# Weight preparation, value loads and planned order of a fused top-k attention and FFN kernel

## The chip, the cores and the metric

The kernel runs on one core of a Trainium2 chip. The core has TensorE (PE; its weight loads are PEld in the profile), VectorE (DVE), ScalarE (ACT), GpSimd (POOL) and SyncE (SP), which here issues all DMA. The metric is the device time of one execution in microseconds, as the median of several runs.

## What is computed

Attention that keeps the 32 largest scores of each row, for 4 batches of 8 heads, 576 positions and 64 columns a head, and then two FFNs over the 2304 tokens.

```python
scores = scale * np.matmul(q, k.transpose(0, 1, 3, 2))
kth = np.partition(scores, -top_k, axis=-1)[..., -top_k:-top_k + 1]
scores = np.where(scores >= kth, scores, -1000000000.0)
attn = np.exp(scores - np.max(scores, axis=-1, keepdims=True))
attn = attn / (np.sum(attn, axis=-1, keepdims=True) + 1e-09)
x = np.matmul(attn, v)
h = x @ w_in;  x = np.maximum(0.01 * h, h) @ w_out
h = x @ w_in2
g = np.where(h >= 1, h, np.where(h <= -1, 0.0, (h + 1) ** 2 / 4.0))
return g @ w_out2
```

The inner width of an FFN is 2048, the outer 512. The result is float32.

## The kernel before

**Units.** Each batch's head has 512 queries in two halves of 256 (`a` = 0, 1) and 64 that are left over. A unit ("m") is one head and one half: scores on PE (L688), copied to SBUF by ACT (tile `s`), the top-k on DVE with four MAX8 (L736) and three MATCH_REPLACE8 (L740) for each of two tiles of 128 queries, the exponential on ACT (`e`, L755 and L756), the division by the sum on POOL (L763), the transposes on PE (L775, copied by ACT to `ptr`), and the product with the values on PE (L859, `pv`). Batch 0 runs all heads of the first half before those of the second, and so loads its values twice. In batches 1 to 3 both halves of a head follow each other. Scores of left-over queries are computed early (`scores_kept`, L712) and come back from DRAM in "r" units. For batches 2 and 3 the transposed left-over rows wait in `rk` and `re` and join the product of the second half (`own` in `pv`).

**Numbers.** PE multiplies a short float type (float32r), so an operand is cut into a high part (ACT casts) and a low one (POOL subtracts): `split`, whose instructions carry L491 and L507. Heads of batches 0 and 1 (`lean_of`) keep their values in float32: `v_whole` loads 128 columns that hold one head's 64 columns twice, and the unit copies out the half that it needs.

**Weights.** The weights arrive as 64-bit floats, 32 blocks of 128 x 512 for each of the two FFNs (layers `L` 0 and 1). `prep_w` makes float32 of each: ACT scales the upper word into `va` (L577), with the exponent placed so that a shift by 3 puts it where it belongs; ACT writes 16 further bits of the mantissa into `bits` (L579); POOL writes the sign, as 0 times the value in bfloat16, into the upper half of `bits` (L584); DVE shifts `va` and joins both (L590). Then the block is cut in two (`px`) and written to DRAM (`scr`). `va` lies in a PSUM bank for the first 16 blocks of layer 0 and in `wa` after that. `bits` is a tile `wb`, of which there are two; it is free again when POOL's subtraction has read it.

**FFN.** `Rows` multiplies rows of batches 0 to 2 (L1032 to L1034 and L1104 to L1106); its activations go through `gt`, of which there are three. `Wide` takes the 768 rows of batch 3 and of the left-over queries at the end, with seven products in place of eight; its first weights come from sums (DVE, L1297) and lie in `ts`, whose first two places are `tsn` and the other three the buffers of `gt`. `late_split` (L1354) writes into the places of `x`.

**Order.** Every operation is recorded with an engine, a duration and the tiles it uses; `Plan.run` then puts them in order before anything is issued. `forward` simulates the engines with given priorities; `backward` gives new priorities from the time that each operation has to the end. Eight passes are made and the shortest kept. Its durations are constants such as `t_a`, `t_v` and 700 for the joining instruction (L592).

## Time and profile before

| | us |
|---|---|
| median of 3 runs | 1146.84 (1146.72 to 1147.48) |
| the profiled execution | 1147.63 |
| its span, first to last instruction | 1145.8 |
| PE busy | 1098.5 (96%) |
| DVE busy | 929.6 (81%) |
| ACT busy | 895.6 (78%) |
| POOL busy | 831.8 (73%) |
| bytes moved by DMA | 251.11 MB, 219 GB/s on average |

Busy time is the union of the instructions that the profiler saw on an engine. Matmuls overlap each other, so the time from the start of one to the start of the next says what one costs, not its duration. Waits are put down to what ended last. Shares over the whole span average over stages with different limits: attention with the first rows of the FFN up to about 860 us, the wide FFN after that.

### The profile page before, as it was taken

How to read it: one execution, taken by the hardware profiler on the slowest of the kernel's cores; microseconds unless marked ns; L12 is line 12 of the kernel's file. 1: busy time of each engine (PE TensorE's matmuls, PEld its weight loads, DVE VectorE, ACT ScalarE, POOL GpSimd, SP SyncE). 2: the span in 40 equal slices, each digit the busy share in tenths (PEclk: the TensorE clock that was granted, in tenths of full speed). 3: DMA queues.
4: the chain of work that ended last, by engine and by line, in shares of the span. 5: the costliest groups of instructions: out<-in, count | busy, mean ns of one | idle time of the engine just before them, and what ended most of it. 6: DMA issues, size and time to landing. Idle time of an engine off the chain costs nothing.

```text
span 1145.8 us, 18836 instructions
## 1 busy us (share of the span) xinstructions
PE 1098.5 (96%) x5992; PEld 959.5 (84%) x5992; DVE 929.6 (81%) x1826; ACT 895.6 (78%) x2029; POOL 831.8 (73%) x952
## 2 busy tenths in 40 slices
PE   6777997999999999999999999999999999999998
PEld 3556896999888788888888888888888999999987
DVE  7999999999999999999999999999947442047510
ACT  6889999999999898989897899999864543346541
POOL 3445587987799878978777777978779884659721
PEclk9899998999999999999999999999999999999999
DMA  9879897789576647564555464544447654755555
GB/s 330 294 268 334 269 392 265 270 307 378 187 269 229 242 164 221 181 216 161 192 177 202 150 204 147 165 146 135 140 149 263 196 201 167 249 211 182 168 169 179
DMA packets 81778, 251.11 MB, mean 219 GB/s; under 512 B 9104, under 2 KB 21520, under 8 KB 77584
## 3 DMA queue, kind: packets, MB, share of 16 engines
q1 hardware_dynamic: 81680, 249.93, 63.5%
q8 instruction: 47, 0.77, 0.3%
q14 instruction: 51, 0.42, 0.1%
HBM read 206.90 MB, written 42.99 MB: 218 GB/s over the span
## 4 chain that ended last, share of the span: by engine, by line
PE 69%; DVE 14%; ACT 9%; POOL 3%; issue 3%; DMA 1%; SPq 0%; POOLq 0%; ACTq 0%; DVEq 0%
PE bank L1034 14%; PE bank L1032 14%; PE bank L1033 14%; DVE m L736 7%; DVE wk L740 5%; PE bank L859 5%; PE bank L775 4%; PE bank L688 4%; PE bank L1104 3%; PE bank L1105 3%; PE bank L1106 3%; PE bank L1381 2%; PE bank L1382 2%; DVE wb L590 2%; PE bank L1380 2%
## 5 line engine op out<-in xcount | busy, mean ns | idle before, releaser
L736 DVE MAX8 m<-wk 128x8 f32<-128x576 f32 x432 | 308.8, 747 | 0.3
L740 DVE MATCH_REPLACE8 wk<-m,wk 128x576 f32<-128x576 f32 x288 | 212.2, 743 | 0.0
L1032 PE MATMUL bank<-x,ring 128*128 128x512 f32 (+2 forms) x376 | 143.1, 381 | 0.0
L507 POOL TENSOR_TENSOR gt<-gr,gt 128x512 fp32r<-128x512 f32 x96 | 126.9, 1322 | 21.6 <-ACT gt L491 12.3
L1034 PE MATMUL bank<-x,ring 128*128 128x512 f32 (+2 forms) x376 | 137.8, 366 | 0.0
L1033 PE MATMUL bank<-x,ring 128*128 128x512 f32 (+2 forms) x376 | 137.7, 366 | 0.0
L507 POOL TENSOR_TENSOR pt<-ptr,pt 64x128 fp32r<-64x128 f32 (+1 forms) x128 | 111.8, 878 | 26.5 <-ACT pt L491 21.7
L763 POOL TENSOR_SCALAR e<-e,rc 128x576 f32<-128x576 f32 x144 | 109.5, 771 | 17.5 <-DVE rc L761 15.5
L491 ACT COPY s<-bank 128x288 f32<-128x288 f32 x256 | 96.8, 402 | 23.4 <-PE bank L688 21.8
L756 ACT ACTIVATE e<-e,nb 128x576 f32<-128x576 f32 x144 | 111.6, 779 | 2.8 <-POOL nb L749 2.7
L775 PE MATMUL bank<-idt,e 128*128 128x128 f32 (+2 forms) x680 | 104.5, 278 | 9.6 <-POOL e L763 7.2
L736 DVE MAX8 m<-s 128x8 f32<-128x576 f32 x144 | 103.4, 745 | 8.6 <-ACT s L491 8.6
L493 ACT ACTIVATE e<-s,nb 128x576 f32<-128x576 f32 x144 | 108.0, 779 | 1.5
L775 PEld LDWEIGHTS bank<-idt,e 128*128 128x128 f32 (+2 forms) x680 | 82.4, 140 | 28.9 <-POOL e L763 11.7
L740 DVE MATCH_REPLACE8 wk<-m,s 128x576 f32<-128x576 f32 x144 | 106.1, 742 | 0.0
L491 ACT COPY ptr<-bank 128x512 f32<-128x512 f32 (+3 forms) x208 | 97.4, 495 | 11.1 <-PE bank L775 10.3
L688 PE MATMUL bank<-kk,qh 128*128 128x288 f32 x384 | 83.5, 311 | 8.3 <-ACT ptr L491 5.9
L507 POOL TENSOR_TENSOR px<-wb,px 128x512 fp32r<-128x512 f32 x58 | 76.6, 1328 | 17.0 <-ACT px L491 16.8
L859 PE MATMUL bank<-ptr,vl 116*128 116x256 f32 (+1 forms) x320 | 81.6, 395 | 4.6 <-ACT ptr L491 4.4
L688 PEld LDWEIGHTS bank<-kk,qh 128*128 128x128 f32 x384 | 66.1, 191 | 21.0 <-ACT ptr L491 6.9
L1034 PEld LDWEIGHTS bank<-x,ring 128*128 128x128 f32 x376 | 70.7, 188 | 10.8
L1032 PEld LDWEIGHTS bank<-x,ring 128*128 128x128 f32 x376 | 70.8, 188 | 7.3 <-ACT gr L493 0.2
(173 smaller groups left out, 3280.6 us busy)
## 6 DMA issues: line engine op xcount, KB each, us to landing
ring<-scr SPq DMA_DIRECT2D x244, 512.0 KB, 3.7
scr<-px SPq DMA_DIRECT2D x58, 512.0 KB, 4.5
wraw<-in_moe_w_in_dram SPq DMA_DIRECT2D x16, 1024.0 KB, 7.1
wraw<-in_moe_w_out_dram SPq DMA_DIRECT2D x16, 1024.0 KB, 7.1
vl<-in_vd_dram SPq DMA_DIRECT2D x24, 320.0 KB, 5.3
kraw<-in_km_dram SPq DMA_DIRECT2D x24, 288.0 KB, 5.0
qraw<-in_qm_dram SPq DMA_DIRECT2D x24, 256.0 KB, 4.3
kraw<-in_km_dram SPq DMA_DIRECT2D x16, 320.0 KB, 4.4
```

What stands on the lines that cost most here:

```text
L491: nc.scalar.copy(out=out_(), in_=in_())
L507: lambda: nc.gpsimd.tensor_tensor(out=out_(), in0=in0(), in1=in1(), op=ALU.subtract),
L688: nc.tensor.matmul(ps()[:, 0:HALF], lhsT=qh()[:, at] if plain else qh()[:, part, at], rhs=kk()[:, c0 + c * HALF:c0 + (c + 1) * HALF], star ...
L736: vec(lambda i=i, c=c, src=src: nc.vector.max(out=m()[:, i, c], in_=src()), 664, [(m, (i, r))], [src], pr)
L740: vec(lambda i=i, c=c, src=src, w=ws[i]: nc.vector.match_replace(out=w(), in_to_replace=m()[:, i, c], in_values=src(), imm_value=NEG), 720 ...
L756: P.op("A", 763, lambda i=i, at=at: nc.scalar.activation(out=at(), in_=at(), func=ACTF.Exp, bias=nb()[:, i, 2:3], accum_out=sums()[:, i:i ...
L763: P.op("P", T_NORM, lambda i=i: nc.gpsimd.tensor_scalar(out=e2()[:, i * S:(i + 1) * S], in0=e2()[:, i * S:(i + 1) * S], scalar1=rc()[:, i: ...
L775: nc.tensor.transpose(ps()[0:n, i * 128:(i + 1) * 128], refs[0][0]()[:, c:c + n], idt())
L859: nc.tensor.matmul(out_ps()[:, at], lhsT=vt()[0:lean_rows[j] if lean else KB, j, :], rhs=src(), start=k == 0 and z == 0, stop=k == len(ste ...
L1032: nc.tensor.matmul(ps, lhsT=wh, rhs=xh, start=first, stop=False, skip_group_check=True)
L1033: nc.tensor.matmul(ps, lhsT=wh, rhs=xl, start=False, stop=False, skip_group_check=True)
L1034: nc.tensor.matmul(ps, lhsT=wl, rhs=xh, start=False, stop=last, skip_group_check=True)
```

## The change

- `prep_w`: ACT's scaling becomes a Prelu whose slope for negative values is 2^32, which leaves a bit in the exponent that the shift by 3 moves into the sign's place. POOL's sign instruction goes, for both layers. The low bits go into one of two fixed tiles (`lows`), in turn, whose other halves are zeroed once at the start. The joined block goes to `wa` (three buffers instead of two, and `va` itself outside PSUM); `wb` is no longer a ring of buffers.
- `v_whole` loads the values of heads 2c and 2c+1 side by side, for the even head, and the odd head uses the same tile. `vl` has three buffers instead of four.
- `pv` with `own`: ACT copies the 64 columns of the left-over rows into the tile of the last keys, and one matmul of 320 columns takes the place of one of 64 and one of 256.
- The planner: two gates (`done`) tell it that `ts` in the buffers of `gt`, and `late_split` in those of `x`, come after their last earlier use. `run` makes 21 forward passes, with factors on the durations of ACT, DVE and POOL in `backward` that differ from pass to pass (`CHAIN`). `forward` and `backward` are written anew in part (what waits for a buffer is set aside until one is freed), with the same rules.

```diff
-BUFS = dict(x=2, xraw=2, kk=4, vl=4, vv=4, kraw=3, px=8, vraw=2, qraw=3, qh=2, s=6, wk=3, e=2, m8=3, nb=3, sums=2, rc=2,
-            pt=3, ptr=3, xb=2, rk=4, re=2, t=3, gr=2, gt=3, wraw=2, wa=2, wb=2)
+BUFS = dict(x=2, xraw=2, kk=4, vl=3, vv=4, kraw=3, px=8, vraw=2, qraw=3, qh=2, s=6, wk=3, e=2, m8=3, nb=3, sums=2, rc=2,
+            pt=3, ptr=3, xb=2, rk=4, re=2, t=3, gr=2, gt=3, wraw=2, wa=3)
...
-EARLY = ("wraw", "wa", "wb", "px")
+EARLY = ("wraw", "wa", "px")
...
-T_SIGN = 795
-SIGNP = (0, 1)
...
+    def done(self, tag):
+
+        uses = {i for i, o in enumerate(self.ops) for r in o[6] if r.tag == tag}
+        self.ops.append(("X", 0, lambda: None, 0.0, uses, [], []))
+        return len(self.ops) - 1
...
     def run(self):
+        self.links()
         prio = [o[3] for o in self.ops]
-        refs = {ref for o in self.ops for ref in o[6] if ref.tag in self.bufs}
-        self.span = None
-        for _ in range(PASSES):
-            for ref in refs:
-                ref.slot = None
+        best = None
+        for z in range(len(CHAIN) + 1):
             span, order = self.forward(prio)
-            if self.span is None or span < self.span:
-                self.span, self.order = span, order
-                slots = [(ref, ref.slot) for ref in refs]
-            began = {i: t for t, i in order}
-            prio = self.backward(began)
+            if best is None or span < best[0]:
+                best = span, order, [(ref, ref.slot) for ref in self.holder]
+            if z < len(CHAIN):
+                prio = self.backward({i: t for t, i in order}, dict(zip("AVP", CHAIN[z])))
+        self.span, self.order, slots = best
...
+CHAIN = (
+    (1.0, 1.0, 1.0), (1.011, 1.025, 0.896), (1.081, 0.936, 1.0), (1.081, 1.033, 1.032), (1.0, 1.058, 0.895),
...
+    (0.98, 0.885, 1.032), (0.99, 0.957, 0.955), (1.0, 0.883, 1.0), (1.031, 1.0, 0.945), (1.007, 0.993, 1.0),
+)
 SLACK = 2500.0
-PASSES = 8
 SLOWER = 1.05
...
-    zero = fixed([128, 1], F32, "zero")
+    lows = [fixed([128, DM], I32, f"low{i}", lambda: pools["wb"]) for i in range(2)]
...
-        vec(lambda: nc.vector.memset(zero(), 0.0), 60, [zero], [], -10)
+        for low in lows:
+            vec(lambda low=low: nc.vector.memset(low(), 0), 300, [low], [], -9)
...
-        va = bank(among=VBANK[L], fifo="va") if L == 0 and j < NBANK else new("wa", [128, DM])
-        bits = new("wb", [128, DM], I32)
+        bits = new("wa", [128, DM])
+        va = bank(among=VBANK[L], fifo="va") if L == 0 and j < NBANK else bits
+        low = lows[j % 2]
         n = DM
-        act(va, lambda: raw()[:, z * 2 * n:(z + 1) * 2 * n].bitcast(F32)[:, 1::2], 560, [va], [raw], pr,
-            scale=2.0 ** -112)
-        act(lambda: bits().bitcast(U16)[:, 0::2] if L in SIGNP else bits(), lambda: raw()[:, z * 2 * n:(z + 1) * 2 * n].bitcast(U16)[:, 1::4],
-            560, [(bits, 0)], [raw], pr, scale=2.0 ** -13, bias=-0.49994)
-        signs = [(3, ALU.logical_shift_left)]
-        if L in SIGNP:
-            P.op("P", T_SIGN, lambda: nc.gpsimd.tensor_scalar(
-                out=bits().bitcast(BF16)[:, 1::2], in0=raw()[:, z * 2 * n:(z + 1) * 2 * n].bitcast(F32)[:, 1::2],
-                scalar1=zero()[:, 0:1], scalar2=1.0, op0=ALU.mult, op1=ALU.mult), w=[(bits, 1)], r=[raw, zero], prio=pr)
-        else:
-            signs.append((-(2 ** 31), ALU.bitwise_and))
-        for shift, op in signs:
-            vec(lambda shift=shift, op=op: nc.vector.scalar_tensor_tensor(
-                out=bits(), in0=va().bitcast(I32), scalar=shift, in1=bits(), op0=op, op1=ALU.bitwise_or),
-                t_v(n) if L == 0 and j < NBANK else 700, [bits], [va, bits], pr)
+        act(lambda: va().bitcast(F32), lambda: raw()[:, z * 2 * n:(z + 1) * 2 * n].bitcast(F32)[:, 1::2], 560, [va], [raw], pr,
+            func=ACTF.Prelu, scale=2.0 ** -112, alpha=2.0 ** 32)
+        act(lambda: low().bitcast(U16)[:, 0::2], lambda: raw()[:, z * 2 * n:(z + 1) * 2 * n].bitcast(U16)[:, 1::4],
+            620, [low], [raw], pr, scale=2.0 ** -13, bias=-0.49994)
+        vec(lambda: nc.vector.scalar_tensor_tensor(
+            out=bits().bitcast(I32), in0=va().bitcast(I32), scalar=3, in1=low(), op0=ALU.logical_shift_left, op1=ALU.bitwise_or),
+            t_v(n) if va is not bits else 700, [bits], [va, low], pr)
...
-            return v_whole(b, h, pr)
+            return v_whole(b, h // 2, pr) if h % 2 == 0 else v_cur[b, h - 1]
...
-    def v_whole(b, h, pr):
+    def v_whole(b, c, pr):
 
         vt = new("vl", [128, NJ, 2 * D])
-        dma(vt, lambda: vd[b, h], 320, [vt], [], pr + 0.5)
+        dma(vt, lambda: vd[b, c], 320, [vt], [], pr + 0.5)
...
             if own:
                 c0 = own["i"] * 128 + own["e"] * REM
-                steps.append(([own["ends"]], [(NJ - 1, lambda: own["ends"]()[:, c0:c0 + REM])]))
-            steps.append(([pt], [(NJ - 1, lambda pt=pt: pt()[:, 0, 0:w])]))
+                act(lambda pt=pt: pt()[:, 0, w:n], lambda: own["ends"]()[:, c0:c0 + REM].bitcast(F32), t_a(REM), [(pt, "own")], [own["ends"]], pr)
+            steps.append(([pt], [(NJ - 1, lambda pt=pt: pt()[:, 0, 0:n])]))
         out_ps = bank(pr)
         for k, (refs, blocks) in enumerate(steps):
-            at = slice(256, 320) if own and k == len(steps) - 2 else slice(0, 256) if own and k == len(steps) - 1 else slice(0, n)
-            def mm(k=k, blocks=blocks, at=at):
+            def mm(k=k, blocks=blocks):
                 for z, (j, src) in enumerate(blocks):
-                    nc.tensor.matmul(out_ps()[:, at], lhsT=vt()[0:lean_rows[j] if lean else KB, j, :], rhs=src(),
-                                     start=k == 0 and z == 0, stop=k == len(steps) - 1 and z == len(blocks) - 1,
-                                     skip_group_check=own is not None)
-            cost = 4 * w / 2.4 if lean else max(T_LEAST, t_m(at.stop - at.start))
-            pe(mm, cost * len(blocks), [out_ps], refs + [vt], pr)
+                    nc.tensor.matmul(out_ps()[:, 0:n], lhsT=vt()[0:lean_rows[j] if lean else KB, j, :], rhs=src(),
+                                     start=k == 0 and z == 0, stop=k == len(steps) - 1 and z == len(blocks) - 1)
+
+            pe(mm, (4 * w / 2.4 if lean else t_m(n)) * len(blocks), [out_ps], refs + [vt], pr)
...
-                split(lambda a, x=x: x()[:, a], t, 512, x, [t], 0, hi, t_pp, t_aa)
+                split(lambda a, x=x: x()[:, a], t, 512, x, [t], 0, hi, t_pp, t_aa, () if L == 0 and i == 0 else (gt_done[0],))
...
-            act(lambda: gd()[:, :, 0], g1, t_aa(2 * HW), [(gd, (e, 0)) for e in range(2)], [g1], lo)
+            act(lambda: gd()[:, :, 0], g1, t_aa(2 * HW), [(gd, (e, 0)) for e in range(2)], [g1], lo, after=(x_done[0],))
...
+        gt_done.append(P.done("gt"))
+        x_done.append(P.done("x"))
...
-    data.append(("vd", np.concatenate([vd, vd], axis=4)))
+    data.append(("vd", np.concatenate([vd[:, ::2], vd[:, 1::2]], axis=4)))
```

## Rows read from the trace of the kernel before

**Rows 1.** The page: the span, and PE's busy tenths in forty slices.
```profile
span 1145.8 us, 18836 instructions
...
PE   6777997999999999999999999999999999999998
```

**Rows 2.** Table by stretches; stretch and length, busy us of each engine, clock, DMA.
```profile
core 0: us, PE busy (x) PEld busy (x) DVE busy (x) ACT busy (x) POOL busy (x), PEclk, DMA share, GB/s
0.00:229.00 229.00, 187.86 (x1057) 156.15 (x1058) 218.70 (x456) 202.44 (x462) 139.30 (x173) 0.96 0.84 302
229.00:430.00 201.00, 198.67 (x1141) 173.37 (x1140) 199.40 (x382) 186.63 (x408) 164.92 (x181) 1.00 0.70 253
430.00:860.00 430.00, 429.93 (x2315) 366.47 (x2314) 396.87 (x833) 373.31 (x900) 344.94 (x459) 1.00 0.53 172
860.00:1117.00 257.00, 257.00 (x1375) 242.98 (x1374) 114.10 (x156) 128.62 (x255) 177.09 (x139) 1.00 0.61 201
```

**Rows 3.** The same table, columns as in group 2, for three early stretches.
```profile
0.00:29.00 29.00, 17.64 (x59) 11.65 (x60) 22.00 (x51) 19.95 (x43) 9.91 (x16) 0.94 0.92 331
...
172.00:201.00 29.00, 21.18 (x119) 17.59 (x117) 27.90 (x57) 27.13 (x61) 21.42 (x26) 0.88 0.72 266
201.00:229.00 28.00, 27.10 (x199) 25.54 (x200) 26.60 (x55) 27.07 (x59) 26.09 (x27) 1.00 0.76 267
```

**Rows 4.** Waits of PE from 0 to 229: us, times, longest.
```profile
PE bank L688 <- DMA qraw<-in_qm_dram: 11.1, 4, 4.2
PE bank L775 <- POOL e L763: 7.2, 9, 2.7
PE bank L688 <- ACT ptr L491: 6.7, 4, 4.2
```

**Rows 5.** Timeline of PE near 857 us: start us, us, what.
```profile
857.08 0.45 PE L859 MATMUL bank<-pt,vv 128*128 128x320 f32 x2
857.37 0.19 PE L859 MATMUL bank<-re,vv 128*128 128x64 f32 x1
...
857.72 0.40 PE L1105 MATMUL bank<-ring,gt 128*128 128x512 f32 x1
...
858.19 0.28 PE L859 MATMUL bank<-pt,vv 128*128 128x256 f32 x1
858.31 0.39 PE L1104 MATMUL bank<-ring,gt 128*128 128x512 f32 x1
858.54 0.40 PE L1105 MATMUL bank<-ring,gt 128*128 128x512 f32 x1
```

**Rows 6.** Groups of instructions by form: xcount | busy us, mean ns | idle before.
```profile
L584 POOL TENSOR_SCALAR wb<-wraw,zero 128x512 bf16<-128x512 f32 x64 | 56.1, 889 | 9.4 <-DMA wraw<-in_moe_w_in_dram 8.5
...
L590 DVE SCALAR_TENSOR_TENSOR wb<-wa,wb 128x512 int32<-128x512 int32 x48 | 49.9, 1046 | 2.7 <-POOL wb L584 1.7 <-ACT nb L747 0.5 <-ACT wb L493 0.3
...
L493 ACT ACTIVATE wa<-wraw 128x512 f32<-128x512 f32 x48 | 32.7, 681 | 0.3 <-PE bank L712 0.3
...
L493 ACT ACTIVATE gr<-bank 128x512 f32<-128x512 f32 x48 | 29.3, 614 | 0.1
...
L491 ACT COPY t<-bank 128x512 f32<-128x512 f32 x30 | 17.5, 594 | 17.9 <-PE bank L1382 16.1 <-PE bank L1034 0.8 <-PE bank L1106 0.7
...
L590 DVE SCALAR_TENSOR_TENSOR wb<-bank,wb 128x512 int32<-128x512 int32 x16 | 10.6, 680 | 0.7 <-ACT wb L493 0.5 <-POOL wb L584 0.2
...
L491 ACT CAST pt<-rk 128x128 fp32r<-128x128 f32 x32 | 9.9, 309 | 0.0
```

**Rows 7.** Timeline, three engines: the last MAX8, a weight split, the first wide product.
```profile
836.11 1.41 DVE L736 MAX8 m<-wk 128x8 f32<-128x576 f32 x2
...
879.36 1.60 POOL L507 TENSOR_TENSOR tsn<-tf,tsn 128x512 fp32r<-128x512 f32 x1
...
888.95 0.33 PE L1032 MATMUL bank<-xa,tsn 128*128 128x384 f32 x1
```

**Rows 8.** DMA issues: tile, count, KB each, median us to landing.
```profile
vl<-in_vd_dram SPq DMA_DIRECT2D x24, 320.0 KB, 5.3
```

More of the change, by code (lines that the diff above doesn't have):

```diff
@@ L192, in backward @@
                     _, i = heapq.heappop(q)
-                    ns = max(500.0, self.took(i, began[i])) if eng == "SP" else self.took(i, began[i])
+                    ns = self.took(i, began[i]) * speed.get(eng, 1.0)
+                    ns = max(500.0, ns) if eng == "SP" else ns
                     late[i] = now + ns + (2100.0 if eng == "SP" else 0.0)
@@ L249, in forward, with push, wake @@
         slots = {t: {i: 0.0 for i in range(c)} for t, c in self.bufs.items()}
+        now, cnt, dma_free = 0.0, 0, 0.0
+        ready_at, ready, events, busy, order, parked = [0.0] * n, {}, [], {}, [], {}
         def slot(ref):
-            if ref.fifo and given.get(ref.fifo, 0) != ref.seq:
-                return None
+            late = SLACK if ref.loaded else 0.0
             free = slots[ref.tag]
-            if ref.loaded:
-                free = {i: t + SLACK for i, t in free.items()}
-            can = [i for i in (ref.among or free) if free.get(i, 1e18) <= now]
+            can = [i for i in (ref.among or free) if free.get(i, 1e18) + late <= now]
             return min(can, key=free.get) if can else None
-        ready_at = [0.0] * n
-        ready = {}
-        events = []
-        busy = {}
-        dma_free = 0.0
-        order = []
-        for i in range(n):
-            if not left[i]:
-                ready.setdefault(self.ops[i][0], []).append((prio[i], i))
-        now, cnt = 0.0, 0
-        for q in ready.values():
-            q.sort()
+        def push(t, what):
+            nonlocal cnt
+            heapq.heappush(events, (t, cnt, what))
+            cnt += 1
+        def wake(key):
+            for i in parked.pop(key, ()):
+                bisect.insort(ready[self.ops[i][0]], (prio[i], i))
         def start(i):
-            nonlocal dma_free, cnt
-            eng, ns, new = self.ops[i][0], self.took(i, now), self.ops[i][5]
-            for ref in new:
+            nonlocal dma_free
+            eng, ns = self.ops[i][0], self.took(i, now)
+            for ref in self.ops[i][5]:
                 ref.slot = slot(ref)
@@ L293, in start @@
-                cnt += 1
-            heapq.heappush(events, (end, cnt, i))
-            cnt += 1
-        def pick(eng):
-            q = ready.get(eng)
-            if not q:
-                return None
-            for k, (_, i) in enumerate(q):
-                ok = ready_at[i] <= now
-                if ok:
-                    new = self.ops[i][5]
-                    ok = all(slot(r) is not None for r in new) and all(
-                        r.slot is not None or r.tag not in self.bufs or r in new for r in self.ops[i][6]
-                    )
-                if ok:
-                    del q[k]
+                push(now + ns, i)
@@ new lines, in pick @@
+        def pick(eng):
+            q, k = ready[eng], 0
+            while k < len(q):
+                i = q[k][1]
+                if ready_at[i] > now:
+                    k += 1
+                    continue
+                key = None
+                for ref in self.ops[i][5]:
+                    if ref.fifo and given.get(ref.fifo, 0) != ref.seq:
+                        key = ref.fifo
+                        break
+                    if slot(ref) is None:
+                        key = "free " + ref.tag
+                        break
+                else:
+                    new = self.ops[i][5]
+                    for ref in self.placed[i]:
+                        if ref.slot is None and ref not in new:
+                            key = ref.fifo or ref
+                            break
+                del q[k]
+                if key is None:
@@ L310, in pick @@
                     return i
+                parked.setdefault(key, []).append(i)
             return None
+        for i in range(n):
+            ready.setdefault(self.ops[i][0], [])
+            if not left[i]:
+                ready[self.ops[i][0]].append((prio[i], i))
+        for q in ready.values():
+            q.sort()
         done = 0
         while done < n:
-            for eng in list(ready):
+            for eng in ready:
                 while busy.get(eng, 0.0) <= now:
@@ L1267, in rest @@
             chunk(3)
+    gt_done, x_done = [], []
     class Wide:
```

106 lines of the change are left out of this document (52 added, 54 removed), and 2 rows, old and new, of the table CHAIN.

## The prediction, as it was made before the result was known

> **What bounds the kernel now.** I read the views from coarse to fine. The page gives a span of 1145.8 us and TensorE (PE) busy in nearly all of it [rows 1]; the profiled execution took 1147.63 us, so 1.83 us lie outside the span. That execution is 0.79 us above the median of the three runs (1146.84), and I carry the sum from the profiled one to the median by that step.
>
> The table by stretches is the view that decides [rows 2]. From 0 to 229 us PE is busy 187.86 us, so it stands idle for 41.1. From 229 to 430 it is idle for 2.3, from 430 to 860 for 0.07, from 860 to 1117 not at all. Everything after 229 us is therefore a PE that always has the next matmul at hand. Only two things can shorten that part: less PE work, or an earlier start because the first 229 us left less undone. VectorE (DVE), which finds the 32 largest scores, is nearly as full: 218.7 of 229, 199.4 of 201 and 396.9 of 430. It is the second bound, not the first. Its last MAX8 ends at 837.5. The first product of the wide FFN starts on PE at 888.95, while the second of the two weight splits that this product and the next one need ends on GpSimd (POOL) at 880.96 [rows 7]. PE comes to that product late because it is still working off the rows of the FFN of batch 2. So about 8 us can be taken from PE's work or idle time before that point without the top-k having to end earlier; past 8 us, DVE must give as well.
>
> The 41.1 us are spread over the first eight stretches: 11.4 in the first, 7.8 in that from 172 to 201, 0.9 in the next [rows 3]. PE's waits there name loads of q (11.1 us in 4 waits, the longest 4.2), POOL's normalised e (7.2) and ScalarE's (ACT) copies of the transposes (6.7) [rows 4]. None of the long ones names the prepared weights.
>
> **The change part by part.**
>
> *The sign of the weights.* Each of 64 weight blocks loses one POOL instruction of 889 ns mean, 56.1 us in all [rows 6]. POOL is busy 139.3 of 229 us in the first stretch and 164.9 of 201 in the second [rows 2], so it is no bound there; DVE's instruction that joins the pieces waited for POOL's sign 1.7 us in total in its larger form and 0.2 us in its smaller one [rows 6]. On the path the removal itself is worth 0 to 2 us, and I take 1. ACT's scaled copy (wa<-wraw, 681 ns) becomes a Prelu with an immediate slope. The nearest row is the Prelu gr<-bank, also without a bias tile: 614 ns against 594 for a plain copy of the same shape [rows 6], so +20 ns x 64 = 1.3 us of ACT in 410 us, behind the same waits as before. Nothing on the path: 0 to 1 us, I take 0. The Trainium skill (ScalarE: Activation LUTs, section What ACT_TABLE_LOAD costs) says that an operand read per partition adds about 93 ns to an activation; if the Prelu took its zero bias that way, the sum would have 64 x 93 = 6 us more of ACT, an estimate from that page, and the row of gr<-bank speaks against it.
>
> The low half is now written into one of two fixed tiles, which are free again when DVE has read them, and no longer when POOL's subtraction is over. ACT's wait behind that subtraction goes. The joined block lies in three buffers instead of two. The two tiles are filled with zeros once on DVE before the first scores; DVE's 16 larger reads of 512 columns from a bank took 680 ns each [rows 6], so at most 1.4 us, and DVE has nothing to do before the first score lands. If that cover were gone it would cost 1.4.
>
> *What the removed POOL work does to DVE.* The joining instruction takes 680 ns when one input is in PSUM (16 times) and 1046 on average when both are in SBUF (48 times) [rows 6]. The difference, 366 x 48 = 17.6 us, is time that DVE, the second bound, loses. The change keeps the two SBUF inputs. In the stretch from 229 to 430, POOL would fall from 164.9 to about 139 us of 201 (some 30 signs go), which is 16% less chance of meeting it: 0.16 x 17.6 = 2.8 us of DVE, bounds 0 and 17.6. It only shows once PE has gained more than the 8 us above, so 0 in the sum. The Trainium skill (SBUF — State Buffer, section Who interferes with whom) says that a DVE instruction with two SBUF inputs and a POOL instruction that reads SBUF lock each other out for a whole instruction. The two rows agree, 680 against 1046 ns, and by that rule the loss shrinks but stays.
>
> *Values in pairs.* Of 24 loads of 320 KB [rows 8] 12 go, 8 of them in batch 0. A load of 320 KB at the 331 GB/s of the first stretch [rows 3] is about 1 us of transfer. The pair needs its bytes for the first head already, so before PE's waits for q only one load less lies in the queue. PE's instructions are the same. 0 to 2 us, I take 0.5. SyncE's queue, which issues all loads, has 12 issues less. A pair holds one of three buffers over two heads; if a value came late, PE would wait before a PV product, and the next head's scores would be queued behind it.
>
> *Last keys joined.* Sixteen times (batches 2 and 3, second half of the queries) a 64-column and a 256-column matmul become one of 320. PE is full there, so its spacing counts. From the 64-column matmul to the second matmul after it 0.35 us pass, with one matmul of 512 columns (0.23) between; that leaves 0.12. The 256-column one takes 858.19 to 858.31, 0.12. Two of 320 columns take 857.08 to 857.37, 0.145 each [rows 5]. 0.12 + 0.12 - 0.145 = 0.095 us x 16 = 1.5 us less PE, bounds 1 and 2. ACT gets 16 copies of 64 columns more; the nearest row, 128 columns, is 309 ns [rows 6], so at most 4.9 us in the 430 us where ACT is busy 373 [rows 2]. They run beside POOL's two subtractions for the same block, and cost the path nothing.
>
> *The planner's two new gates.* The transformed weights of the second wide step share buffers with gt and now stand, in the planned order, behind the last use of any gt. Until that use and the split behind it are over, PE has the 42 products of the first wide step. 0 to 1 us, I take 0.
>
> *The order.* All else is the same work in another order: the forward planner runs 21 times instead of 8, with weights of time for DVE, ACT and POOL that differ from pass to pass, and keeps the shortest plan. After 229 us there is nothing for it to win on PE. Before, its room is the 41.1 us, of which the wait for the first loads and the lack of any FFN work before the first four head pairs are done cannot go. What an order can mend is a stretch like that from 172 to 201: in its longest wait PE stood 4.2 us for a copy of a transpose that ACT had queued behind weight preparation and a softmax [rows 3, 4], while the stretch after it lost 0.9. The difference, about 7, is the upper bound of what it can win there, and the same 7 is what it can lose if it makes a second stretch of that kind. I take 2 gained. The granted clock in the first 229 us is 0.96 on average [rows 2], 0.04 x 187.9 = 7.5 us of PE; a PE that idles less may get a part of that back, 0 to 3, I take 0.
>
> Sum: 1 + 0.5 + 1.5 + 2 = 5.0 us less, 1142.6 against the profiled 1147.63 and 1141.8 against the median. I forecast **1142**.
>
> **The rivals.**
>
> *No change.* Every stretch before 229 us keeps its idle time, since the waits named there are loads, ACT and POOL's e and not the sign. Only the joined keys count, less the tighter gate: -1.5 + 0.5 = -1, about 1146. For it: none of the long waits names what the change removes. Against it: all three engines besides PE get a different order.
>
> *Slower, by a stall of ACT's queue.* With POOL free, the order can bring weight preparation forward; each block puts three activations (two of about 0.7 to 0.8 us and a cast) into ACT's queue, ahead of the copies that empty PE's banks. ACT was already busy 202.4 of 229 us [rows 2]. One more stretch like that from 172 to 201 costs 7 us, two cost 14: 1146.8 - 2 + 7 = 1152 for one. It decides as soon as PE's idle time before 229 us rises above 43 us (41.1 and the 2 us of the other parts). Speaking for it: that stall exists today. Against: DVE and ACT have no more to do than before.
>
> *Much faster.* If the search finds a feed for PE that halves the 41.1, PE gains 15 to 20; the 8 us of slack before the first wide product and about 3 us of DVE's cap it at 11 and the joined keys add 1.5: 1134. It needs PE's idle time before 229 us at 30 or under, and the last MAX8 before 835.
>
> **How the numbers follow.** The forecast with its neighbours (2.3 to 10 us faster) has 0.50, much faster 0.11, no change 0.20, the stall 0.19. A measurement of this kernel tells about 0.2% (2.3 us) from no change. So faster 0.61, same 0.20, slower 0.19. The range takes the forecast, no change, the cap of much faster down to 1134 and the stall up to 1151; about a tenth lies under it and a tenth above.
>
> **What would show it.** PE's idle time before 229 us should be 36 to 39 us and nearly nothing after it. The sign's group on POOL (56.1 us) is gone and POOL's busy time is near 776. The joining instruction with two SBUF inputs still averages over 900 ns; at 700 the lock was the sign's doing. The value loads are 12. The 64-column matmuls are gone, and the end of the last MAX8 has moved by under 5 us. The prediction is wrong if PE's idle time before 229 us moves by more than 8 us either way, if PE shows idle time between 430 and 1117, or if ACT's Prelu takes 750 ns or more.

## The result and the profile after

The changed kernel takes 1137.85 us (median; 1137.27 to 1138.94) against 1147.48 for the kernel before: a ratio of 0.9916 (0.9905 to 0.9927), 9.6 us less. The forecast was 1142 with a range from 1134 to 1151. The direction is right and the time lies in the range, but the gain is nearly twice the 5.0 us of the sum.

The page of the changed kernel: span, PE's busy time, PE's busy tenths [rows 1].

```profile
span 1136.3 us, 18693 instructions
...
PE 1096.7 (97%) x5976; PEld 960.7 (85%) x5976; DVE 917.4 (81%) x1827; ACT 897.8 (79%) x2045; POOL 775.9 (68%) x888
...
PE   6797998999999999999999999999999999999998
```

The table by stretches of the changed kernel (us of the stretch and its length, then busy us of each engine with its instructions, granted clock, DMA share, GB/s), to be held against [rows 2]:

```profile
0.00:229.00 229.00, 193.75 (x1091) 161.44 (x1092) 218.18 (x457) 203.06 (x463) 112.95 (x141) 0.96 0.83 291
229.00:430.00 201.00, 200.44 (x1139) 175.62 (x1138) 194.61 (x383) 188.37 (x411) 140.78 (x154) 1.00 0.71 255
430.00:860.00 430.00, 430.00 (x2306) 367.42 (x2305) 398.49 (x838) 379.33 (x922) 345.47 (x460) 1.00 0.52 172
860.00:1108.00 248.00, 248.00 (x1338) 236.20 (x1338) 105.56 (x151) 122.48 (x246) 171.17 (x134) 1.00 0.61 201
```

**Where the time went.** PE's idle time is the span less its busy time: 1145.8 - 1098.5 = 47.3 us before, 1136.3 - 1096.7 = 39.6 after. So 7.7 us of the 9.5 in the span are idle time and 1.8 are busy time. The idle time fell from 41.1 to 35.25 up to 229 us, and from 2.3 to 0.56 up to 430. From 430 us on PE stands for less than 0.1 us in either kernel. The same reading by count: up to 430 us PE had done 1057 + 1141 = 2198 matmuls before and 1091 + 1139 = 2230 now. Of all its matmuls 5976 - 4536 = 1440 are left at 860 us, where 5992 - 4513 = 1479 were left before; 39 at (1145.8 - 860) / 1479 = 0.193 us each are 7.5 us.

The same table in other stretches; first the changed kernel, then the rows of the kernel before that [rows 3] does not hold:

```profile
0.00:115.00 115.00, 88.30 (x385) 65.14 (x385) 108.10 (x234) 92.58 (x222) 32.48 (x55) 0.96 0.84 279
...
0.00:29.00 29.00, 18.43 (x63) 13.59 (x64) 22.57 (x53) 16.06 (x36) 2.06 (x8) 0.94 0.91 323
...
57.00:86.00 29.00, 25.45 (x121) 18.48 (x119) 29.00 (x62) 25.73 (x65) 9.22 (x15) 1.00 0.82 272
...
143.00:172.00 29.00, 26.66 (x164) 23.33 (x163) 28.12 (x58) 28.54 (x65) 19.43 (x23) 0.94 1.01 406
172.00:201.00 29.00, 25.36 (x157) 23.25 (x156) 26.42 (x54) 27.41 (x60) 22.47 (x22) 0.88 0.72 248
```

```profile
0.00:115.00 115.00, 83.13 (x361) 61.24 (x362) 107.20 (x231) 95.52 (x224) 50.66 (x75) 0.94 0.86 306
...
57.00:86.00 29.00, 21.73 (x107) 16.50 (x108) 29.00 (x61) 25.75 (x64) 12.21 (x20) 1.00 0.80 269
...
143.00:172.00 29.00, 29.00 (x218) 27.78 (x217) 29.00 (x54) 26.67 (x62) 25.51 (x27) 1.00 1.00 389
```

From 172 to 201 us PE wins 4.2 us, and from 143 to 172 it loses 2.3 that it did not lose before. The largest lasting gain is earlier: from 57 to 86 us PE is busy 25.45 us instead of 21.73.

PE's waits from 0 to 229 us in the changed kernel (us, times, longest), against [rows 4]:

```profile
PE bank L698 <- DMA qraw<-in_qm_dram: 9.8, 2, 5.4
PE bank L785 <- POOL e L773: 6.9, 12, 1.6
PE bank L698 <- ACT s L508: 4.4, 5, 2.7
PE bank L698 <- ACT xraw L508: 3.6, 4, 2.3
```

ACT's copies of the transposes (6.7 us in [rows 4], longest 4.2) are no longer among the first. The loads of q and POOL's e are.

Groups of instructions by form in the changed kernel (xcount | busy us, mean ns | idle before), against [rows 6]:

```profile
L600 DVE SCALAR_TENSOR_TENSOR wa<-wa,low 128x512 int32<-128x512 int32 x48 | 42.5, 894 | 2.0 <-ACT low L510 1.7 <-ACT wa L510 0.2
...
L510 ACT ACTIVATE wa<-wraw 128x512 f32<-128x512 f32 x48 | 32.6, 690 | 0.8 <-POOL px L524 0.8
...
L867 PE MATMUL bank<-pt,vv 128*128 128x320 f32 x144 | 28.0, 309 | 0.0
...
L600 DVE SCALAR_TENSOR_TENSOR wa<-bank,low 128x512 int32<-128x512 int32 x16 | 10.8, 676 | 0.4 <-POOL ring L524 0.4
```

Timelines of the changed kernel (start us, us, what): the last MAX8, the second weight split, the first wide products, against [rows 7]:

```profile
831.72 1.42 DVE L746 MAX8 m<-wk 128x8 f32<-128x576 f32 x2
```

```profile
878.49 1.28 POOL L524 TENSOR_TENSOR tsn<-tf,tsn 128x512 fp32r<-128x512 f32 x1
```

```profile
880.00 0.33 PE L1038 MATMUL bank<-xa,ring 128*128 128x384 f32 x1
...
881.06 0.34 PE L1038 MATMUL bank<-xa,tsn 128*128 128x384 f32 x1
```

The last MAX8 ends at 833.1 instead of 837.5. PE comes to the wide FFN at 880.0 instead of 888.95, and 256.3 us follow until the end of the span (256.9 before). The second split ends at 879.8, 1.3 us ahead of the first product that reads `tsn`: the 8 us between these two are used up.

### The profile page after: what moved, and what is told of

Same layout as the page of the kernel before. It is cut to its first block, busy times and chain, and to the rows that moved or that the text cites. A ratio compares the mean times of both kernels' runs of the same rounds, so it can differ in the third digit from the quotient of the medians.

```text
span 1136.3 us, 18693 instructions
## 1 busy us (share of the span) xinstructions
PE 1096.7 (97%) x5976; PEld 960.7 (85%) x5976; DVE 917.4 (81%) x1827; ACT 897.8 (79%) x2045; POOL 775.9 (68%) x888
## 4 chain that ended last, share of the span: by engine, by line
PE 86%; DVE 8%; ACT 5%; issue 1%; POOL 0%; DMA 0%; SPq 0%; POOLq 0%
PE bank L1040 17%; PE bank L1038 17%; PE bank L1039 17%; PE bank L867 7%; PE bank L785 6%; PE bank L698 5%; DVE m L746 4%; PE bank L1110 4%; PE bank L1112 4%; PE bank L1111 4%; DVE wk L750 3%; PE bank L1390 2%; PE bank L1389 2%; PE bank L1388 2%; ACT e L766 1%; PE bank L884 1%
## 5 line engine op out<-in xcount | busy, mean ns | idle before, releaser
L773 POOL TENSOR_SCALAR e<-e,rc 128x576 f32<-128x576 f32 x144 | 107.2, 755 | 19.0 <-DVE rc L771 14.0
L524 POOL TENSOR_TENSOR px<-wa,px 128x512 fp32r<-128x512 f32 x58 | 77.2, 1339 | 25.2 <-ACT px L508 22.7
L1040 PEld LDWEIGHTS bank<-x,ring 128*128 128x128 f32 x376 | 70.8, 188 | 10.7
L769 POOL TENSOR_TENSOR rc<-sums,tiny 128x2 f32<-128x2 f32 x72 | 14.2, 197 | 93.5 <-ACT e L766 87.6
L867 PE MATMUL bank<-ptr,vl 116*128 116x256 f32 (+1 forms) x320 | 77.3, 382 | 0.7 <-ACT ptr L508 0.6
```

The lines of the kernel that those rows point to most:

```text
L524: lambda: nc.gpsimd.tensor_tensor(out=out_(), in0=in0(), in1=in1(), op=ALU.subtract),
L867: nc.tensor.matmul(out_ps()[:, 0:n], lhsT=vt()[0:lean_rows[j] if lean else KB, j, :], rhs=src(), start=k == 0 and z == 0, stop=k == len(st ...
L1040: nc.tensor.matmul(ps, lhsT=wl, rhs=xh, start=False, stop=last, skip_group_check=True)
```

## The experiments

Each kernel is timed against the kernel before on the same chip; the ratios carry 95% intervals. "The planner's own reckoning" is the length of the plan that it kept, from its fixed durations. It is 1147.79 us for the kernel before and 1144.47 for the changed one (the 15th of 21 passes).

### The search alone

All the work of the kernel before, under the new planner with its gates and 21 passes.

```diff
...
-        bits = new("wa", [128, DM])
+        bits = new("wb", [128, DM], I32)
...
-            return v_whole(b, h // 2, pr) if h % 2 == 0 else v_cur[b, h - 1]
+            return v_whole(b, h, pr)
...
-            steps.append(([pt], [(NJ - 1, lambda pt=pt: pt()[:, 0, 0:n])]))
+            steps.append(([pt], [(NJ - 1, lambda pt=pt: pt()[:, 0, 0:w])]))
```

> The work of the kernel before (sign on POOL, values of single heads, last keys apart) with the planner of the changed kernel, its 21 passes and its two gates. Theory A (the gain is idle time of PE before 229 us that a better order fills, and the longer search finds such an order for any work): 1140 to 1143. Theory B (POOL's freed time is the gain, whatever the order): 1147, as before. Theory C (the factors of the search fit the work that they were looked for with, and do nothing for another): 1146 to 1151.

1150.9 us, 1.0026 (1.0015 to 1.0037): 3 us slower than before. The page of this kernel:

```profile
PE 1105.0 (96%) x5992; PEld 961.4 (84%) x5992; DVE 934.3 (81%) x1826; ACT 895.6 (78%) x2029; POOL 831.0 (72%) x952
```

For this work the longer search is worth nothing; its best plan was reckoned at 1149.98, longer than the 1147.79 of the eight plain passes. It is the plan of the second of the 21 passes, the last that no factor has touched yet: no pass with factors made a shorter one. That is what theory C expected, and theory A is refuted for these factors. The same 5992 matmuls also take 6.5 us more of "busy" time than before (1098.5): some waiting is counted as busy and not seen as idle. PE's idle time up to 229 us even fell, to 37.45 us from 41.1:

```profile
0.00:229.00 229.00, 191.55 (x1054) 158.23 (x1055) 216.27 (x454) 201.80 (x461) 139.41 (x172) 0.96 0.84 301
```

### The new work under the old search

```diff
-CHAIN = (
-    (1.0, 1.0, 1.0), (1.011, 1.025, 0.896), (1.081, 0.936, 1.0), (1.081, 1.033, 1.032), (1.0, 1.058, 0.895),
...
+CHAIN = ((1.0, 1.0, 1.0),) * 7
```

> The work of the changed kernel (no sign on POOL, pairs of values, last keys joined), planned with eight passes without factors, as many as before. Theory A: the gain is mostly gone, 1144 to 1148, and PE's idle time before 229 us is back at about 41. Theory B: the gain stays, 1138 to 1140. Theory C: 1146 or more, since this work has only a poor order without the factors.

1151.16 us, 1.0021 (1.0009 to 1.0034); reckoned at 1151.79. With all three edits of the work and none of the factors the kernel is slower than before, as theory C expected; theory B, that POOL's freed time is the gain whatever the order, is refuted. Neither the new search on the old work nor the new work under the old search gains. Here too PE's idle time up to 229 us is less than before, 37.5 us:

```profile
0.00:229.00 229.00, 191.51 (x1069) 159.90 (x1070) 215.63 (x454) 202.81 (x459) 110.38 (x138) 0.93 0.83 291
```

### The sign left out in the old order

The order, the buffers and the activations of the kernel before, with POOL's sign instruction left out and nothing in its place, so the weights lose their sign. The Prelu, the two fixed tiles and the third buffer of `wa` are not in this kernel.

```diff
...
-            P.op("P", T_SIGN, lambda: nc.gpsimd.tensor_scalar(
...
+            P.op("P", T_SIGN, lambda: None, w=[(bits, 1)], r=[raw, zero], prio=pr)
```

> The kernel before in its own order, with POOL's sign instruction left out and nothing put in its place, so the weights lose their sign: 56 us less on POOL and one wait less for DVE, all else as it was. Theory A: 1145 to 1147, since none of PE's long waits names the sign. Theory B: 1138 to 1141.

1145.24 us, 0.9971 (0.9961 to 0.9981): 3.3 us less, in an order that was made for the sign, and within what theory A expected. Its row of the table from 229 to 430 us and its joining instruction:

```profile
229.00:430.00 201.00, 200.62 (x1159) 176.54 (x1159) 194.63 (x387) 189.32 (x414) 141.45 (x154) 1.00 0.71 257
```

```profile
L593 DVE SCALAR_TENSOR_TENSOR wb<-wa,wb 128x512 int32<-128x512 int32 x48 | 39.5, 830 | 5.5 <-ACT wb L582 5.3
```

PE does 1159 matmuls there instead of 1141 [rows 2]; 18 more at 0.193 us each are 3.5 us, more than the 2.3 us that PE stood idle. A view that the prediction did not read points to the reason: the chain of waits, cut to 229 to 430 us (shares by engine and line). The kernel before:

```profile
by line: DVE m L736 9.6%; issue 8.6%; DVE wk L740 6.9%; DVE wb L590 5.4%; POOL px L507 5.2%; PE bank L1032 4.3%; PE bank L1033 4.3%; PE bank L1034 4.1%; POOL wb L584 4.1%; ACT e L756 3.9%; POOL gt L507 3.7%; PE bank L859 3.2%; ACT wb L493 3
```

The same without the sign:

```profile
by line: PE bank L862 15.1%; PE bank L1035 14.7%; PE bank L1037 14.6%; PE bank L1036 14.6%; PE bank L778 8.7%; PE bank L1107 7.3%; PE bank L1109 7.3%; PE bank L1108 7.3%; PE bank L691 7.3%; ACT s L491 1.2%; ACT e L759 0.8%; ACT e L493 0.7%;
```

And the changed kernel:

```profile
by line: PE bank L1038 15.3%; PE bank L1040 15.0%; PE bank L1039 15.0%; PE bank L867 14.0%; PE bank L698 8.1%; PE bank L785 7.7%; PE bank L1112 7.1%; PE bank L1110 7.1%; PE bank L1111 7.1%; ACT e L766 0.8%; ACT ptr L508 0.7%; ACT t L508 0.7
```

Before, the chain ran through the top-k, the joining (5.4% of 201 us, 11 us) and POOL's sign (4.1%, 8 us), although PE stood only 2.3 us there. Without the sign it runs almost through PE alone. The shares are no prices: the sign stood in the chain for 8 us and leaving it out gave 3.3. What DVE's shorter joins and POOL's shorter queue give of the 3.3 us was not told apart.

### The sign put back into the new order

```diff
...
+            nc.gpsimd.tensor_scalar(
+                out=low().bitcast(BF16)[:, 1::2], in0=raw()[:, z * 2 * n:(z + 1) * 2 * n].bitcast(F32)[:, 1::2],
+                scalar1=zero()[:, 0:1], scalar2=1.0, op0=ALU.mult, op1=ALU.mult)
```

The order of the changed kernel stays; POOL writes the sign into the upper half of `low` behind ACT's low bits. The planner does not know of the instruction.

> The changed kernel in its own order, with POOL's sign instruction issued again for each of the 64 blocks, into the upper half of the low tile, so that DVE waits for it as before. Theory A: 1138 to 1141, as this order has its gain from PE's feed. Theory B: 1145 to 1148. Besides, DVE's joining instruction with two SBUF inputs should go back from 894 ns towards 1046 if it was the sign that it met on the shared port.

1154.55 us, 1.0058 (1.0043 to 1.0073): against 0.9916 for the changed kernel 0.0142 x 1147.5 = 16 us slower. A row of its table, one of DVE's waits from 0 to 430 us, and the joining instruction:

```profile
229.00:430.00 201.00, 195.10 (x1120) 169.80 (x1120) 190.06 (x368) 182.89 (x394) 163.41 (x176) 1.00 0.68 247
```

```profile
DVE wa L612 <- POOL low L607: 10.8, 10, 2.0
```

```profile
L612 DVE SCALAR_TENSOR_TENSOR wa<-wa,low 128x512 int32<-128x512 int32 x48 | 45.7, 957 | 11.3 <-POOL low L607 10.8 <-ACT low L605 0.3
```

Both theories expected a shorter time, 1148 us at most. The new order cannot bear the sign: DVE stands 10.8 us for POOL, where it stood 1.9 before [rows 6], and PE does 1120 matmuls in this stretch instead of 1139.

### More and less work of one engine, in the new order

Three kernels ask which engine is the bound in batches 2 and 3, after 430 us: 39 MAX8 of batches 2 and 3 made twice, 39 of their MATCH_REPLACE8 taken away, and 128 transposes made twice.

```diff
...
+                more = 2 if r == 3 and i == 0 and n == 2 and u_batch[0] >= 2 else 1
...
+                    for _ in range(more):
+                        nc.vector.max(out=m()[:, i, c], in_=src())
```

```diff
...
+                less = r == 2 and i == 0 and n == 2 and u_batch[0] >= 2
...
+                    if not less:
```

```diff
...
-            for i, (c, n) in enumerate(blocks):
+            for i, (c, n) in enumerate(blocks + (blocks if twice else [])):
...
```

> The changed kernel in its own order, with one more MAX8 (the fourth of one tile done twice) in each of the 39 units of batches 2 and 3: 39 x 0.66 = 26 us more on DVE between 430 and 833 us, nothing else. Theory P (after 229 us PE is the bound and DVE has some slack, of which the changed kernel kept 1 to 4 us; DVE's own idle moments, some 16 us there, take up a part): 5 to 14 us slower. Theory D (DVE's top-k is the bound, and PE's full busy time hides short stalls): 22 to 27 us slower.

> The changed kernel in its own order, with the third MATCH_REPLACE of one tile left out in the same 39 units (so the fourth MAX8 finds the same eight as the third, and the threshold of those rows is another): 39 x 0.73 = 28 us less on DVE there. Theory P: 0 to 3 us faster, since PE has no less to do. Theory D: 10 us faster or more, until PE becomes the bound.

> The changed kernel in its own order, with the four transposes of the first two key blocks done twice in the units of batches 2 and 3 whose tiles are turned together: 32 x 4 x 0.109 = 14 us more on PE between 430 and 850 us. Theory P: 12 to 15 us slower. Theory D: 0 to 6 us slower.

Measured: 1152.99 us, 1.0038 (1.0022 to 1.0055) with 27.4 us more of DVE (944.8 - 917.4 busy); 1138.91, 0.992 (0.9902 to 0.9938) with 22.6 us less; 1151.8, 1.0031 (1.0022 to 1.0041) with 12.3 us more of PE (1109.0 - 1096.7 busy). The row from 430 to 860 us of each, in that order:

```profile
430.00:860.00 430.00, 423.94 (x2234) 353.73 (x2234) 419.62 (x869) 367.23 (x899) 332.77 (x446) 1.00 0.50 167
```

```profile
430.00:860.00 430.00, 430.00 (x2305) 367.09 (x2304) 375.65 (x760) 378.93 (x920) 345.51 (x458) 1.00 0.51 173
```

```profile
430.00:860.00 430.00, 430.00 (x2369) 369.87 (x2368) 391.70 (x826) 371.56 (x901) 334.77 (x446) 1.00 0.50 168
```

PE's extra work arrives whole (12.0 us in the span, 1148.3 - 1136.3, for 12.3; by the ratios it is 13). Less DVE work buys nothing that can be told: the medians are 1138.91 and 1137.85. So PE is the bound of the changed kernel where the work was added, from 430 us on. Between 229 and 430 us this was not tried; there its chain runs almost through PE alone (above). The second bound is close: of 27.4 us more on DVE 14.9 arrive in the span (1151.2 - 1136.3), by the ratios 14, the upper end of theory P. So about 12 of them find room, and PE then stands 6 us between 430 and 860.

### Another pass, and more passes

The 18th of the 21 passes in place of the 15th, and, in a second kernel, 44 triples of factors in place of 20, which makes 45 passes.

```diff
...
-            if best is None or span < best[0]:
+            if z == 17:
...
```

> The work of the changed kernel with the order of another pass, the 18th of the 21, which the planner holds to be 0.3 us longer than the one it kept (1144.74 against 1144.47 by its own reckoning). If orders that it holds to be equal are equal on the chip: 1137 to 1140. If the kept order is a lucky draw among equals: 1141 to 1146.

> The changed kernel with 45 passes instead of 21, whose factors were looked for until the planner held the order to be 4.2 us shorter (1140.28 against 1144.47). If a shorter plan is a shorter run: 1130 to 1135, with PE's idle time before 229 us under 33. If the planner's reckoning is worn out at this size: 1136 to 1141.

1138.24 us, 0.9915 (0.9898 to 0.9933), for a plan reckoned at 1144.74; and 1137.92, 0.9919 (0.9905 to 0.9933), for one reckoned at 1140.28. The chip does not tell the three apart: the gain does not hang on the one plan that was kept, and 4.2 us less in the reckoning (1144.47 - 1140.28) gave nothing. A row of the second, up to 229 us:

```profile
0.00:229.00 229.00, 196.43 (x1099) 163.93 (x1099) 220.08 (x457) 203.49 (x464) 110.23 (x140) 0.93 0.84 287
```

The granted clock is 0.93 here and 0.96 in the changed kernel, at the same time of execution. Its chain of waits from 229 to 430 us has the top-k on DVE in it again, with no loss of time:

```profile
by line: PE bank L1044 9.8%; PE bank L1043 9.7%; PE bank L872 9.7%; PE bank L1045 9.6%; PE bank L1117 6.8%; PE bank L1115 6.8%; PE bank L1116 6.8%; PE bank L790 5.5%; DVE m L751 4.9%; PE bank L703 4.7%; DVE wk L755 3.6%; ACT e L771 2.4%; DV
```

### The sign kept, and planned anew

Pairs, joined keys and the 21 passes as in the change; the weights as in the kernel before, with the ring of `wb` and without the fixed tiles.

```diff
...
-            func=ACTF.Prelu, scale=2.0 ** -112, alpha=2.0 ** 32)
+            scale=2.0 ** -112)
...
+            P.op("P", T_SIGN, lambda: nc.gpsimd.tensor_scalar(
...
```

> The changed kernel with POOL's sign instruction and the ring of wb as in the kernel before, and values in pairs and joined keys as changed, planned anew with the 21 passes. The planner holds its order to be 1.5 us longer than that of the changed kernel (1145.99 against 1144.47). If the gain needs POOL's freed time (e4 put the same instruction back without planning anew, and lost 16 us): 1143 to 1149. If a plan that knows of the sign does as well: 1138 to 1141.

1146.14 us, 0.9987 (0.9978 to 0.9996): 1.5 us less than before (0.5 to 2.5 by the interval), as much as the joined keys were taken to be worth; that it is the joined keys was not tested here. Planned at 1145.99, which the fourth of the 21 passes gave. With the sign, the search finds an order with a full stretch from 229 to 430 us, but with the first one as empty as before in matmuls:

```profile
0.00:229.00 229.00, 192.38 (x1042) 156.53 (x1043) 216.94 (x446) 200.93 (x457) 139.89 (x172) 0.93 0.83 291
229.00:430.00 201.00, 200.06 (x1153) 175.94 (x1152) 195.40 (x386) 187.88 (x407) 164.68 (x180) 1.00 0.70 249
```

1042 + 1153 = 2195 matmuls up to 430 us, against 2198 before and 2230 in the changed kernel.

### The last keys apart again

```diff
...
+                    if own and k == len(steps) - 1:
+                        for at in (slice(256, 320), slice(0, 256)):
+                            nc.tensor.matmul(out_ps()[:, at], lhsT=vt()[0:KB, j, :], rhs=src()[:, at],
+                                             start=False, stop=True, skip_group_check=True)
...
```

> The changed kernel in its own order, with the joined matmul of 320 columns issued as one of 64 and one of 256 again (16 times), nothing else. PE is the bound there and the spacing says 0.095 us each: 1.5 us slower (1 to 2), so 1139 to 1140.5. If the joining is worth nothing: no difference.

1139.17 us, 0.9932 (0.9918 to 0.9945), against 0.9916 for the changed kernel: 0.0016 of 1147.5, 1.8 us. PE's busy time is 2.2 us higher (1098.9). The two intervals overlap, and the profiled span is only 0.2 us longer (1136.5), so the 1.5 us agree with the medians but are not proved.

### The loads back

Each load of a pair is followed by a second transfer of the same 320 KB, into DRAM.

```diff
...
+            nc.sync.dma_start(out=spare[0], in_=vd[b, c])
...
```

> The changed kernel in its own order, with each of the 12 loads of a pair of values followed by one more transfer of the same 320 KB, from DRAM to DRAM, that nobody reads: the bytes and the issues of the 12 loads that the change saves. If the pairs are worth what was taken for them: 0.5 us slower (0 to 2). If the loads of q, on which PE waits at the start, come later by it: 2 to 5 us slower.

1138.07 us, 0.9919 (0.9906 to 0.9933): 12 transfers of the same size on the same queue cost nothing that can be told. What they do not undo is the number of buffers of `vl`.

## Why the prediction was right, and where its sizes were not

The time fell into the range and the bound was named rightly for most of the span. The sum was not right: the sign was sized too small, and half of the gain comes neither from the sign alone nor from the search alone. The range held because the rivals had made it wide, not because of the prices of the terms. The times, the work done up to 430 us, and the planner's reckoning side by side:

| | ratio | matmuls up to 115 us | 115 to 229 | 229 to 430 | sum | reckoned |
|---|---|---|---|---|---|---|
| kernel before | 1 | 361 | 697 | 1141 | 2199 | 1147.79 |
| search alone | 1.0026 | 361 | 694 | 1128 | 2183 | 1149.98 |
| new work, old search | 1.0021 | 363 | 709 | 1113 | 2185 | 1151.79 |
| old order, no sign | 0.9971 | 357 | 700 | 1159 | 2216 | - |
| new order, sign back | 1.0058 | 362 | 673 | 1120 | 2155 | - |
| sign kept, planned anew | 0.9987 | 357 | 688 | 1153 | 2198 | 1145.99 |
| changed kernel | 0.9916 | 385 | 709 | 1139 | 2233 | 1144.47 |
| another pass | 0.9915 | 392 | 708 | 1138 | 2238 | 1144.74 |
| more passes | 0.9919 | 366 | 733 | 1140 | 2239 | 1140.28 |

(A matmul that spans a border counts on both sides, hence 2199 for 2198 and 2233 for 2230.) The sums rank the kernels nearly as their times do. PE's idle time up to 229 us, which the prediction took as its sign, does not: it is 41.1 us before, 37.45 in the search alone and 37.5 under the old search, both slower than before, and 37.6 with another pass, which is as fast as the changed kernel with its 35.25. The changed kernel's 34 more, at 0.193 us each, are 6.6 us of its 9.6; the joined keys, 1.5, come after 430 us.

**What bounds the kernel: right from 430 us on.** PE alone, so that only less PE work or an earlier start can gain; DVE second, with some 8 us to give. The runs with more PE and less DVE show it for the changed kernel, and the 8 us were used nearly to the last. From 229 to 430 us it does not hold for the kernel before: the old order without the sign gains there, though PE had stood idle for only 2.3 us. The cap of the "much faster" rival, 11 + 1.5 us, held: the result lies 3 us under it. Its conditions were half met: the last MAX8 is before 835, PE's idle time before 229 us is 35.25 and not 30.

**The sign, 0 to 2 us with 1 taken: too small.** In the old order it is worth 3.3 (2.2 to 4.5 by the interval). The step that failed is the one that says of POOL "so it is no bound there", and takes DVE's 1.7 us of waits for the sign as all that the sign costs. PE's waits and DVE's waits name only who came last. The chain from 229 to 430 us had POOL's sign, the joining and POOL's subtraction in it for 4.1, 5.4 and 5.2%, and this stretch is where the old order without the sign gained.

**DVE's relief, 2.8 us of DVE, put at 0 in the sum: as DVE time too small as well.** The joining instruction with two inputs in SBUF fell from 1046 to 894 ns: 152 x 48 = 7.3 us. The prediction scaled the excess with POOL's busy share, 16% less; it fell by 152 / 366 = 42%. The check that it "still averages over 900 ns" was missed narrowly. That it shows only past 8 us is doubtful for the stretch before 430 us, where DVE was in the chain; what the 7.3 us are worth in the kernel's time was not measured.

**The order, 2 us with 7 as the bound: mis-sized, and with the wrong place.** The text said that the first loads and the missing FFN work set the early stretches, and looked for a gain from 172 to 201. That stretch gained 4.2, but with its neighbours from 115 to 229 us only 0.7 is left (idle 9.3 to 8.55). Up to 115 us idle time fell by 5.2 (31.87 to 26.7). One piece of independent PE work shows how: `scores_kept`, 64 matmuls that wait for loads and no top-k. Their rows, first the kernel before, then the changed one (durations, first and last start):

```profile
L712 PE MATMUL bank<-wa x32: 403/406/510, 17.1 to 147.8; 128*128 128x288 f32 x32
```

```profile
L722 PE MATMUL bank<-wa x32: 403/407/511, 13.7 to 119.1; 128*128 128x288 f32 x32
```

46 of the 64 start before 115 us in the kernel before, 62 in the changed one, 62 and 64 with another pass and with more; 50 with the sign kept. They can fill gaps that PE had anyway, which is argued from the counts. Weight preparation gives way: POOL's first `px` starts at 31.4 us instead of 12.5, and POOL is busy 2.06 us of the first 29 instead of 9.91 [rows 3]. Early scores alone are not enough, though: the new work under the old search starts 56 before 115 us, the new order with the sign 60, and both lose more matmuls after 115 us than they win before it (the table).

**What neither term held: 4.8 us, whose cause stays open.** Removing the sign alone gives 3.3 us; the search with the sign kept, joined keys included, gives 1.5; both give 9.6, so 9.6 - 3.3 - 1.5 = 4.8 us belong to neither. Every plan made without the sign starts its first `px` late (30.8 to 31.4 us in four of them) and every plan made with it early (12.5 to 13.3 in three), under either search; that the shorter path is what allows the late start is argued from this, not shown. The late start alone does not pay: under the old search it came with a slower kernel. The prediction added the parts as if each had its own price. Two other readings of the 4.8 us stand. The factors may fit the work that they were looked for with, and not the absence of the sign as such (theory C): on the old work no factor shortened the plan, and whether other factors would find an equal order with the sign kept was not tried. An order alone moves more than 4.8 us: the new work under the old search is 0.0050, nearly 6 us, slower than the old order without the sign. And the two fixed tiles and the third buffer for the joined blocks are in neither of the two kernels that are summed here, so their share lies in the 4.8 as well.

**Joined keys, 1.5: in agreement** with the apart run (1.8, not proved) and with 16 matmuls less (5976 for 5992). **Pairs, 0.5: no more than the measurement tells**; the value loads are 12. **Gates, clock and zeros at 0:** nothing in the trace speaks against them; the granted clock stayed 0.96 before 229 us.

**The other checks.** PE's idle time before 229 us is 35.25, just under the 36 to 39 expected, and two slower kernels would have met that check (above); POOL is busy 775.9 (776); the Prelu takes 690 ns against 681 for the scaled copy (under 750); the last MAX8 moved by 4.4 us (under 5). PE stands nowhere between 430 and 1108. The 93 ns for a bias per partition that the Trainium skill (ScalarE: Activation LUTs, What ACT_TABLE_LOAD costs) gives are not seen in these 9 ns.

**The rivals.** *No change* is nearly what these factors gave with the sign kept (0.9987). *Slower by ACT's queue* did not come: ACT is as busy up to 229 us as before (203.06 for 202.44), and the long wait for a transpose's copy is gone. Slower orders are near, all the same: three of the kernels with half of the change are slower than before.

## What to carry to other kernels

When a step is to be taken out of a preparation chain, read the chain of waits of the stretch in which it runs, not only the waits of the engine that bounds the kernel: a nearly full PE can hide that the chain runs through others. The chain says where to look and not what a removal is worth. An edit that shortens a side chain and a new order of the work need not add up (4.8 of 9.6 us here); price them together, time the edit alone and the search alone, and look for the order anew for each before calling the rest a joint effect. To compare orders of the same work, count the bounding engine's instructions up to a fixed time: the counts ranked nine kernels nearly as their times did, where idle time did not.

## What the runs showed of the hardware that was not expected

The joining instruction on DVE (128x512, two inputs in SBUF) has no fixed price. It took 1046, 991, 1000 and 957 ns in the four kernels with POOL's sign (before, search alone, sign kept, sign back), and 830, 948 and 894 in three without it (old order, old search, changed kernel), while the form with one input in PSUM stayed at 672 to 682 ns. Two rows each of DVE and POOL in the changed kernel show what it hangs on:

```profile
371.36 1.29 POOL L524 TENSOR_TENSOR px<-wa,px 128x512 fp32r<-128x512 f32 x1 [0.38 <-ACT px L508]
371.48 1.72 DVE L600 SCALAR_TENSOR_TENSOR wa<-wa,low 128x512 int32<-128x512 int32 x1
...
397.74 0.67 DVE L600 SCALAR_TENSOR_TENSOR wa<-wa,low 128x512 int32<-128x512 int32 x1
...
398.62 0.20 POOL L759 TENSOR_TENSOR nb<-nb 128x2 f32<-128x2 f32 x1 [2.65 <-ACT nb L757]
```

The first join starts 0.12 us after a subtraction of POOL and takes 1.72 us; the second runs while POOL stands and takes 0.67. Of the 48 joins those that POOL's instructions overlap for less than 0.1 us took 666 to 694 ns, in the kernel before (8 of them) as in the changed one (11). The Trainium skill (SBUF — State Buffer, Who interferes with whom) says that DVE and GpSimd share one pair of ports under an exclusive lock; these rows agree, and the mean moves with the order alone: 1046 and 991 ns for the old work, 948 and 894 for the new.

PE's busy time is no measure of its work: with the same 5976 matmuls it was 1096.7 us in the changed kernel and 1105.9 with more work on DVE, so some 9 us that no further matmul explains are counted as busy there.

At the same work a granted clock of 0.93 up to 229 us (more passes) and one of 0.96 (changed kernel) go with equal times, 1137.92 and 1137.85 us. The orders differ, so this does not show what the clock costs there; it shows that the lower mean did not come out as a loss.
